# Masked attention with a rational feed-forward on one core: weights decoded without a sign operation, half visits that load their query columns alone, V's padding cleared on GpSimd, and a new order

## The chip, the cores and the metric

The kernel runs on one core of a Trainium2 chip. A core has five engines that run in parallel, each with its own queue of instructions in a fixed order: PE (matrix products; the profile shows its weight loads apart, as PEld), DVE (VectorE), ACT (ScalarE), POOL (GpSimd) and SP (SyncE), which here only issues transfers. The metric is the time of the launch in microseconds of the device, the median of several runs.

## The reference

Attention over 8 batches of 8 heads, 576 positions of 64 values, in which all scores further than tau below their row's maximum are dropped, and a feed-forward layer with a rational function in the middle:

```python
scores = scale * np.matmul(q, k.transpose(0, 1, 3, 2))
thresh = np.max(scores, axis=-1, keepdims=True) - tau
scores = np.where(scores >= thresh, scores, -1000000000.0)
scores = scores - np.max(scores, axis=-1, keepdims=True)
attn = np.exp(scores)
attn = attn / (np.sum(attn, axis=-1, keepdims=True) + 1e-09)
x = np.matmul(attn, v)          # then laid out as 4608 rows of 512
...
h = x @ w_in                    # 512 to 2048
P = a[0] + a[1] * h + a[2] * h2 + a[3] * h3
Q = 1.0 + np.abs(b[0]) * np.abs(h) + np.abs(b[1]) * h2
out = (P / (Q + 1e-06)) @ w_out # 2048 to 512
```

The two weight matrices are handed over as 64-bit floating-point words, which the kernel turns into 32-bit ones itself. Everything else is 32-bit.

## The kernel before

**Attention.** Heads are taken in pairs, 4 pairs to a batch, 32 in all. A pair's 576 rows are four tiles of 128 and a rest of 64; a pair of heads and a tile make a unit. For a unit PE forms the scores (L806, the rest L796), DVE takes the negated maximum (L814), ACT or DVE makes the threshold from it and tau (L821, L823), ACT applies it with a Prelu of a huge slope (L829) and takes the exponential with its sum (L833). The sum is scaled on ACT or DVE (L838, L840) and inverted on DVE (L844). For most units the result is then split into a high and a low half-precision part (high by `times`, L343 on ACT and L345 on DVE; low on DVE, L855), both are transposed by DMA from SP's queue (L865), and PE multiplies them with V (L924). In the first batch many units go another way: DVE scales the identity by the inverted sums (L871), PE transposes by a product with it (L878, L883), `copy` brings the result out (L335 on ACT, L337 on DVE), and PE multiplies in 32 bits (L908). The result is split again into x (L934 or L936, L940).

**Visits.** A pair is not worked through at once. In each batch, three pairs are visited for tiles 0 and 1, the fourth for all five, and then the three again for tiles 2, 3 and the rest: 7 visits a batch, 56 in all, 24 of each half and 8 whole ones. A visit loads its queries (L651, L652, L654 for the rest) and its keys (L659) into one of two buffers each, from SP's queue. Before the change all visits load all query columns.

**V.** V of a pair of heads lies in one of four buffers of 640 columns: four tiles of 128 and 128 more for the rest, of which each head's half is padded by zeros. The buffer is used again for V's half-precision parts, so from the fifth pair on the padding is set to zero anew, on DVE after the load (two memsets, L712). The load is one large DMA (L688) and two small ones (L692), on SP's queue for the first 8 pairs and on GpSimd's afterwards. ACT or DVE takes the largest value (L703, L701), and V is scaled and split (L343 or L345, L741, L744).

**Weights.** 32 pieces of 128 x 512 words are loaded by GpSimd (L549 for w_in, L585 for w_out) and decoded between the units of the first batches. `f1` multiplies the upper half of the word, read as a 32-bit number, by 2^-112 (`times`: ACT L343, DVE L345). `f2` shifts the lower half right on ACT (L507). `f4` shifts the product left by three bits on DVE (L511), which loses its sign. `f5` puts the sign back on DVE (L515). `f6` adds the lower half by an integer addition on DVE (`tensor_tensor`, L350, an ISA row in the order). w_in is then measured (ACT, L557), scaled and split (`times` into `wi`, and L573), w_out split (`copy` into `wp`, and L596).

**Feed-forward.** It goes in steps of 256 rows of x and 512 hidden columns. 48 products L1041 give h (moved by ACT, L1050), ACT and DVE work the rational function (L1055 to L1083), whose result g is split (`copy`, L335 or L337; DVE, L1091), and 24 products L1100 gather the output (L1111, stored by L1120 on GpSimd's queue or, at the end, on SP's). The steps of the last batch's three parts, 12 of them, follow when attention is done.

**The order.** All operations are first entered in a plan: an engine or a choice of engines (`FLEX`, with a duration for each), a key, what must come before, and the buffers it takes and gives back. `Plan.order` then picks the next operation for each engine by a model of times: the smallest key among those that can start first. Where there is a choice, `PRICE` (`EARLY` before `EARLY_END` on the model's clock) weighs the engines. Two tables, `TURN` and `KIND`, shift the keys, by the unit or step and by the kind of operation. In idle gaps of PE up to 400 us on the model's clock, filler products with the identity (L1240) are put in. The engines then run what this gave them, in that order.

Of the kernel before, what the change touches and what calls it, by code (L numbers as in the profile page):

```python
# [8 lines left out]
F32 = mybir.dt.float32  # L9
# [39 lines left out]
NV = 4  # L49
# [24 lines left out]
FLEX = {"f1": {"ACT": 0.567, "DVE": 0.335}, "f6": {"DVE": 0.6}, "s1": {"ACT": 0.648, "DVE": 0.396},  # L74
# [6 lines left out]
EARLY = {"ACT": 1.4369, "DVE": 3.4200}  # L81
EARLY_END = 714.5248
PRICE = {"ACT": 1.0733, "DVE": 2.2524}

TURN = [
# [208 lines left out]
def masked_attention_rational_ffn(  # L294
# [73 lines left out]
    ctx.enter_context(tc.manual_schedule())  # L368
    nc.scalar.preload_act_table_set("natural_log_exp_and_others")
    cf = const.tile([P, 16], F32, name="cf")  # L370
    nc.sync.dma_start(cf[:, 6:7], tau.partition_broadcast(P))
    cv = cf[:, 8:16]
    passes, taue = cv[:, 2:3], cv[:, 3:4]
    ident = const.tile([P, P], F32, name="ident")
# [908 lines left out]
```

## Time and profile before

| | us |
|---|---|
| median of 3 runs (lowest, highest) | 1292.1 (1291.5, 1294.09) |
| the profiled execution | 1291.3 |
| its span, first to last instruction | 1289.5 |
| mean granted TensorE clock | 0.989 |
| DMA queue of SP, share of the 16 DMA engines' time | 44.8% |
| bytes moved | 145.22 MB |

A group of instructions is shown by line, engine, operation, and what it writes and reads, with count, busy time, the mean duration in nanoseconds, and the idle time of its engine just before it, with what ended most of it. Durations of neighbours on one engine overlap a little, so the means times the counts give more than the engine's busy time. A busy PE is not PE at its peak: matmuls are pipelined, and their ends are modelled. An engine's waits are put down to what came last.

### The profile page before, as it was taken

Reading aid. Unit: us, or ns where it says so; the run is one execution under the profiler, and the core shown is the slowest. Engines: PE = TensorE matmul, PEld = TensorE weight load, DVE = VectorE, ACT = ScalarE, POOL = GpSimd, SP = SyncE. Lnnn points to the kernel's source line nnn. Section 1 sums busy time; section 2 is a strip of 40 time slices with the busy share of each in tenths; the row PEclk is TensorE's granted clock in tenths of the full one; section 3 lists DMA queues with packets and bytes.
Section 4 is the critical chain, followed back from the end, with each engine's and each line's share of the span. In section 5 each row is a group of like instructions: output and inputs, shape, how many; then the busy total and the mean of one; then the engine's idle time right before and its main releaser. Section 6 shows DMA issues by size and latency. Waiting matters only on the chain.

```text
span 1289.5 us, 25792 instructions
## 1 busy us (share of the span) xinstructions
PE 1233.6 (96%) x9668; PEld 966.1 (75%) x9668; DVE 1218.6 (95%) x1935; ACT 1110.6 (86%) x2159; POOL 83.8 (6%) x159
## 2 busy tenths in 40 slices
PE   7889899999999999999999989999899999999998
PEld 6667677777777777777777777777677777778886
DVE  5899999999999999899999899999999999999787
ACT  5899999989999989899999799989889899885564
POOL 1111000001001000001000110011001000000000
PEclk8899999999999999999999999999899999999999
DMA  7444374657566565576464465576655665634000
GB/s 207 133 127 130 108 149 92 107 131 155 118 112 143 111 128 111 94 143 145 107 103 101 92 143 113 107 125 123 144 107 121 130 126 108 132 56 72 18 17 16
DMA packets 340779, 145.22 MB, mean 113 GB/s; under 512 B 313136, under 2 KB 318000, under 8 KB 340656
## 3 DMA queue, kind: packets, MB, share of 16 engines
q1 hardware_dynamic: 329840, 111.27, 44.8%
q0 software_dynamic: 10496, 31.73, 8.1%
q8 instruction: 76, 1.25, 0.4%
q10 hardware_dynamic: 320, 0.59, 0.2%
q14 instruction: 47, 0.39, 0.1%
HBM read 58.85 MB, written 9.44 MB: 53 GB/s over the span
## 4 chain that ended last, share of the span: by engine, by line
PE 26%; DVE 22%; issue 5%; ACT 4%; DMA 2%; SPq 0%; DVEq 0%; ACTq 0%
PE banks L1100 11%; PE banks L1041 8%; DVE e L855 4%; PE banks L806 3%; PE banks L924 3%; DVE t L1077 2%; DVE t L1080 2%; DVE st L814 2%; DVE t L1064 2%; DVE g L1091 2%; DVE t L1083 2%; DVE t L1061 2%; DVE t L1074 2%; DMA pT<-hi 1%; PE banks L796 1%
## 5 line engine op out<-in xcount | busy, mean ns | idle before, releaser
L1100 PE MATMUL banks<-wp,g 128*128 128x512 f32 x1728 | 444.3, 405 | 10.7 <-ACT u L1111 7.1
L1100 PEld LDWEIGHTS banks<-wp,g 128*128 128x128 f32 x1728 | 315.0, 189 | 91.7 <-ACT u L1111 7.8
L1041 PEld LDWEIGHTS <-wi 128*128 128x128 f16 x3456 | 328.9, 98 | 72.0 <-issue 30.1
L1041 PE MATMUL banks<-x,wi 128*128 128x256 f16 x3072 | 359.3, 273 | 10.8 <-ACT t L1050 6.8
L833 ACT ACTIVATE e<-e,cf 128x576 f32<-128x576 f32 x288 | 221.1, 774 | 0.2
L829 ACT ACTIVATE e<-banks,st 128x576 f32<-128x576 f32 x288 | 205.8, 735 | 12.4 <-DVE st L823 10.3
L343 ACT ACTIVATE hi<-e,st 128x576 f16<-128x576 f32 x220 | 168.1, 769 | 51.4 <-DVE st L844 45.2
L855 DVE SCALAR_TENSOR_TENSOR e<-e,st,hi 128x576 f16<-128x576 f32 x252 | 204.0, 810 | 4.2 <-ACT hi L343 3.0
L806 PE MATMUL banks<-KK,QQ 64*128 64x64 f32 (+1 forms) x1024 | 175.7, 454 | 10.9 <-ACT e L829 4.4
L814 DVE TENSOR_REDUCE st<-banks 128x2 f32<-128x1152 f32 x128 | 172.1, 1345 | 11.2 <-PE banks L806 9.8
L806 PEld LDWEIGHTS banks<-KK,QQ 64*128 64x128 f32 x1024 | 115.8, 187 | 81.4 <-issue 47.8
L1050 ACT ACTIVATE t<-banks,hsc 128x512 f32<-128x512 f32 (+1 forms) x192 | 106.0, 575 | 25.1 <-PE banks L1041 17.7
L924 PE MATMUL banks<-pT,V 128*64 128x256 f16 (+1 forms) x2520 | 122.3, 250 | 4.4 <-DMA pT<-e 2.1
L924 PEld LDWEIGHTS <-V 128*64 128x64 f16 x2520 | 104.6, 111 | 24.4 <-issue 19.2
L1077 DVE SCALAR_TENSOR_TENSOR t<-t,co,t 128x1024 f32<-128x1024 f32 (+1 forms) x73 | 92.2, 1263 | 16.9 <-ACT t L1071 16.8
L1068 ACT ACTIVATE t<-t,co 128x1024 f32<-128x1024 f32 (+1 forms) x73 | 82.7, 1132 | 28.1 <-DVE t L1074 27.5
L1091 DVE TENSOR_TENSOR g<-t,g 128x512 fp32r<-128x512 f32 x144 | 94.9, 682 | 1.7 <-ACT g L335 1.5
L1061 DVE SCALAR_TENSOR_TENSOR t<-t,co 128x1024 f32<-128x1024 f32 (+1 forms) x73 | 92.1, 1262 | 2.5 <-ACT t L1050 2.5
L1083 DVE SCALAR_TENSOR_TENSOR t<-t,co,t 128x1024 f32<-128x1024 f32 (+1 forms) x73 | 92.3, 1264 | 0.6
L1074 DVE SCALAR_TENSOR_TENSOR t<-t,co,t 128x1024 f32<-128x1024 f32 (+1 forms) x73 | 92.1, 1262 | 0.2
L1064 DVE SCALAR_TENSOR_TENSOR t<-t,co 128x1024 f32<-128x1024 f32 (+1 forms) x73 | 92.1, 1262 | 0.0
L1080 DVE SCALAR_TENSOR_TENSOR t<-t,t 128x1024 f32<-128x1024 f32 (+1 forms) x73 | 87.8, 1203 | 0.6
(118 smaller groups left out, 1202.5 us busy)
## 6 DMA issues: line engine op xcount, KB each, us to landing
KK<-in_kT_dram SPq DMA_DIRECT2D x108, 144.0 KB, 3.0
t<-in_w_in_dram POOLq DMA_DIRECT2D x16, 512.0 KB, 5.7
t<-in_w_out_dram POOLq DMA_DIRECT2D x16, 512.0 KB, 4.8
QQ<-in_qT_dram SPq DMA_DIRECT2D x56, 144.0 KB, 2.8
QQ<-in_qT_dram SPq DMA_DIRECT2D x56, 128.0 KB, 2.8
out_dram<-u POOLq DMA_DIRECT2D x26, 256.0 KB, 3.7
V<-in_v_dram POOLq DMA_DIRECT2D x24, 256.0 KB, 4.7
pT<-hi SPq DMA_TRANSPOSE x140, 3.3
```

Of the source, the lines that this page charges most:

```text
L343: nc.scalar.activation(dst, src, AF.Identity, scale=factor)
L806: mm = nc.tensor.matmul(s[:, d0:d0 + n], QQ[r, t * P:(t + 1) * P], KK[r, k0:k0 + n], **one)
L814: nc.vector.tensor_reduce(box["st"][:, 0:2], box["both"], AX.X, ALU.max, negate=True)
L829: nc.scalar.activation(ev(hh), box["s"][hh], AF.Prelu, scale=SCALE, bias=box["st"][:, 2 + hh:3 + hh], alpha=STEEP)
L833: nc.scalar.activation(e, e, AF.Exp, scale=passes, accum_out=box["st"][:, 4 + hh:5 + hh])
L855: nc.vector.scalar_tensor_tensor(box["lo"][:, c], ev(hh), box["st"][:, 6 + hh:7 + hh], box["hi"][:, c], ALU.mult, ALU.subtract)
L924: nc.tensor.matmul(dst, V[:, c * P + hh * D:c * P + (hh + 1) * D], rhs, start=c == 0 and n == 0, stop=c == NT and n == 2)
L1041: nc.tensor.matmul(d, wi_tile(c, f0 + j, hl), x[:, c, :], start=c == 0 and n == 0, stop=c == NC - 1 and n == 2)
L1077: nc.vector.scalar_tensor_tensor(box["q"], box["q"], qc, box["i"], ALU.add, ALU.mult)
L1083: nc.vector.scalar_tensor_tensor(box["r"], box["r"], a0, box["q"], ALU.add, ALU.mult)
L1091: nc.vector.tensor_tensor(fr(g[:, 1]), box["r"][:, k * GW:(k + 1) * GW], g[:, 0], ALU.subtract)
L1100: nc.tensor.matmul(acc[tt], fr(g[:, x]), fr(wo[f][y]), start=begins and j == n == 0, stop=ends and j == nb - 1 and n == 2)
```

## The change

`f1` is now always on ACT: a Prelu with the scale 2^-112 and, for negative inputs, the slope -2^32. A negative number so becomes positive with an exponent larger by 32, and the shift left by three bits moves that bit of the exponent into the sign. `f5` is gone, and `f1` is no longer in `FLEX`:

```diff
-            times(box["w"], box["rw"][:, :, 1].bitcast(F32), REBIAS)
+            nc.scalar.activation(box["w"], box["rw"][:, :, 1].bitcast(F32), AF.Prelu, scale=REBIAS, alpha=-2.0 ** 32)
...
-        def f5():
-            t = box["w"].bitcast(I32)
-            nc.vector.scalar_tensor_tensor(t, box["rw"][:, :, 1], -0x80000000, t, ALU.bitwise_and, ALU.bitwise_or)
...
-        o1 = op(FLEX["f1"], 0, key, f1, [l], [ht])
+        o1 = op("ACT", 0.567, key, f1, [l], [ht])
         o2 = op("ACT", 0.568, key, f2, [l])
         o4 = op("DVE", 0.335, key, f4, [o1])
-        o5 = op("DVE", 0.602, key, f5, [o4])
-        o6 = op(FLEX["f6"], 0, key, f6, [o5, o2], (), [ht] if dst is None else [ht, hold])
+        o6 = op(FLEX["f6"], 0, key, f6, [o4, o2], (), [ht] if dst is None else [ht, hold])
```

A visit loads the query columns of its own tiles; tau and the four small operations on it (L385 to L388) come behind the first visit's queries:

```diff
         def ldq():
             QQ = QQs[qh.slot]
-            queue.dma_start(QQ[0:D, 0:S], qT[bb, pr, :, 0:S])
-            queue.dma_start(QQ[D:P, 0:NT * P], qT[bb, pr, :, S + REM:])
+            c0, c1 = min(ts) * P, min((max(ts) + 1) * P, NT * P)
+            queue.dma_start(QQ[0:D, c0:S if NT in ts else c1], qT[bb, pr, :, c0:S if NT in ts else c1])
+            queue.dma_start(QQ[D:P, c0:c1], qT[bb, pr, :, S + REM + c0:S + REM + c1])
             if NT in ts:
                 queue.dma_start(QQ[D:P, S:], qT[bb, pr, :, S:S + REM])
+            if first:
+                load_tau()
```

V's padding is cleared by GpSimd for the pairs whose V it loads, ahead of the load:

```diff
+        zero = None if bp < NV else nc.vector if bp < EARLY_BP else nc.gpsimd
+
+        def f_zero():
+            for hh in range(2):
+                zero.memset(Vs[vhold.slot][hh * D:(hh + 1) * D, NT * P + (1 - hh) * D:NT * P + (2 - hh) * D], 0.0)
+
         def ld():
             t = Vs[vhold.slot]
+            if zero is nc.gpsimd:
+                f_zero()
...
-        if bp >= NV:
+        if zero is nc.vector:
             l = v_loaded[bp] = op("DVE", 0.15, max(q, V0 + V1 * pr), f_zero, [l])
```

The tables and prices are others, some 430 numbers:

```diff
-EARLY = {"ACT": 1.4369, "DVE": 3.4200}
+EARLY = {"ACT": 1.2686, "DVE": 3.3582}
-PRICE = {"ACT": 1.0733, "DVE": 2.2524}
+PRICE = {"ACT": 0.8038, "DVE": 2.3173}
...
-    -752, -4167, -3369, 460, -829, -1129, -1318, 524, -372, -1803, -727, -460, -323, 277, -2038, -63, 358, 277, 325,
+    -22753, 3745, 43, -7018, -4551, -3960, -7042, -2152, -4958, -4167, -1023, -845, -1748, -2460, -1722, -1546, 64,
```

So every engine's order is another. Counted over the whole program, DVE has these fewer or more: L515 32 to 0, `times` of the decoding (L345) 16 to 0, memsets 56 to 8, casts of g (L337) 48 to 29, casts of w_out 5 to 13, scalings of w_in (L345) 5 to 13, thresholds (L823) 71 to 61. What has a choice and left DVE is on ACT, and the reverse; the 32 Prelus of `f1` stand there for 16 `times`. GpSimd has 48 memsets more, PE 60 filler products in place of 90.

DVE where the first weights are decoded, before; `u` holds the product of `f1`, `t` the loaded words, and the ISA row is `f6`:

```order
L345 TENSOR_SCALAR u_75<-t_69 128x512
L701 TENSOR_REDUCE vm_272<-V_159 128x1
L511 TENSOR_SCALAR u_75<-u_75 128x512
L871 TENSOR_SCALAR u_74<-ident,st_84 128x128
L515 SCALAR_TENSOR_TENSOR u_75<-t_69,u_75 128x512
L871 TENSOR_SCALAR u_74<-ident,st_84 128x128
L350 ISA t_69<-t_69,u_75 128x512x2
L345 TENSOR_SCALAR u_76<-t_70 128x512
L844 RECIPROCAL st_85<-st_85 128x2
L511 TENSOR_SCALAR u_76<-u_76 128x512
```

The same engine and place now, under the new numbers of the lines (L516 is `f4`, L352 `f6`, L878 the scaled identity):

```order
L516 TENSOR_SCALAR u_74<-u_74 128x512
L516 TENSOR_SCALAR u_76<-u_76 128x512
L352 ISA t_69<-t_69,u_74 128x512x2
L352 ISA t_70<-t_70,u_76 128x512x2
L878 TENSOR_SCALAR u_74<-ident,st_86 128x128
L516 TENSOR_SCALAR u_75<-u_75 128x512
L878 TENSOR_SCALAR u_74<-ident,st_86 128x128
L352 ISA t_71<-t_71,u_75 128x512x2
```

Three rows for a piece (or four, where `f1` was on DVE) have become two, and two pieces are decoded back to back, their `f1` being ACT's.

SP's queue at the start of the program, before:

```order
L371 DMA cf<-in_tau_dram 128x1
L651 DMA QQ_111<-in_qT_dram 64x576
L652 DMA QQ_111<-in_qT_dram 64x512
L688 DMA V_159<-in_v_dram 128x4x128
L692 DMA V_159<-in_v_dram 64x64 x2
L688 DMA V_160<-in_v_dram 128x4x128
L692 DMA V_160<-in_v_dram 64x64 x2
L651 DMA QQ_112<-in_qT_dram 64x576
```

And now (L652 and L653 load queries, L388 tau, L699 and L703 V):

```order
L652 DMA QQ_110<-in_qT_dram 64x256
L653 DMA QQ_110<-in_qT_dram 64x256
L388 DMA cf<-in_tau_dram 128x1
L652 DMA QQ_111<-in_qT_dram 64x256
L653 DMA QQ_111<-in_qT_dram 64x256
L699 DMA V_154<-in_v_dram 128x4x128
L703 DMA V_154<-in_v_dram 64x64 x2
L699 DMA V_155<-in_v_dram 128x4x128
```

Tau went behind the first visit's queries, the second visit's queries went ahead of V's first loads, and each of the first two visits loads 256 columns for each head.

GpSimd's queue where its loads of V begin, behind the last loads of weights, before:

```order
L688 DMA V_162<-in_v_dram 128x4x128
L692 DMA V_162<-in_v_dram 64x64 x2
L1120 DMA out_dram<-u_74 128x512
L1120 DMA out_dram<-u_75 128x512
L1120 DMA out_dram<-t_73 128x512
L688 DMA V_161<-in_v_dram 128x4x128
```

And now (L693 is the memset, L1127 the store of a result):

```order
L1127 DMA out_dram<-u_74 128x512
L1127 DMA out_dram<-u_76 128x512
L693 MEMSET V_155 64x64 x2
L699 DMA V_155<-in_v_dram 128x4x128
L703 DMA V_155<-in_v_dram 64x64 x2
L693 MEMSET V_157 64x64 x2
L699 DMA V_157<-in_v_dram 128x4x128
L703 DMA V_157<-in_v_dram 64x64 x2
```

Two memsets stand ahead of each load of V, and the first stores of results went ahead of the first loads.

More of the change, by code (lines that the diff above doesn't have):

```diff
@@ L72 @@
 RECENT = 9.0
-FLEX = {"f1": {"ACT": 0.567, "DVE": 0.335}, "f6": {"DVE": 0.6}, "s1": {"ACT": 0.648, "DVE": 0.396},
+FLEX = {"f6": {"DVE": 0.6}, "s1": {"ACT": 0.648, "DVE": 0.396},
         "s2": {"DVE": 0.663}, "vmax": {"ACT": 0.697, "DVE": 0.729}, "thr": {"ACT": 0.242, "DVE": 0.122},
@@ L370, in masked_attention_rational_ffn @@
     cf = const.tile([P, 16], F32, name="cf")
-    nc.sync.dma_start(cf[:, 6:7], tau.partition_broadcast(P))
     cv = cf[:, 8:16]
@@ L384, in masked_attention_rational_ffn, with load_tau @@
     KKs = [const.tile([P, S], F32, name=f"KK{i}") for i in range(NQ)]
-    nc.vector.tensor_scalar(passes, cf[:, 6:7], 0.0, None, ALU.is_ge)
-    nc.vector.tensor_scalar(cv[:, 4:5], cf[:, 6:7], 0.0, ALL, ALU.is_lt, ALU.mult)
-    nc.vector.tensor_scalar(taue, cf[:, 6:7], 0.0, 80.0, ALU.max, ALU.min)
-    nc.vector.tensor_tensor(taue, taue, cv[:, 4:5], ALU.add)
+    def load_tau():
+        nc.sync.dma_start(cf[:, 6:7], tau.partition_broadcast(P))
+        nc.vector.tensor_scalar(passes, cf[:, 6:7], 0.0, None, ALU.is_ge)
+        nc.vector.tensor_scalar(cv[:, 4:5], cf[:, 6:7], 0.0, ALL, ALU.is_lt, ALU.mult)
+        nc.vector.tensor_scalar(taue, cf[:, 6:7], 0.0, 80.0, ALU.max, ALU.min)
+        nc.vector.tensor_tensor(taue, taue, cv[:, 4:5], ALU.add)
     b0, b1 = cv[:, 0:1], cv[:, 1:2]
@@ L661, in load_ops @@
         issue = {"DMA": 1.25, "GD": 1.1}[eng]
-        q_done[bp] = [op(eng, 3.1 if first else issue + (0.6 if NT in ts else 0.0), p0, ldq, (), [qh], wire=(0.75, 1.0))]
+        q_done[bp] = [op(eng, 1.8 if first else issue + (0.6 if NT in ts else 0.0), p0, ldq, (), [qh], wire=(0.75 if len(ts) > 3 else 0.4, 1.0))]
         k_done[bp] = [op(eng, 0.1 if act else issue, p0 + 0.1, ldk, (), [kh], wire=(0.75, 1.0))]
@@ L705, in load_v_ops @@
         q = bp * (NT + 0.5) - 17.0
-        l = v_loaded[bp] = op(eng, 1.7, max(q, V0 + V1 * pr), ld, (), [vhold], wire=(0.95, 1.5 if eng == "DMA" else 2.5))
+        l = v_loaded[bp] = op(eng, 1.7 if bp < EARLY_BP else 2.0, max(q, V0 + V1 * pr), ld, (), [vhold], wire=(0.95, 1.5 if eng == "DMA" else 2.5))
         hv = [Hold("u", 1)]
-        def f_zero():
-            for hh in range(2):
-                nc.vector.memset(Vs[vhold.slot][hh * D:(hh + 1) * D, NT * P + (1 - hh) * D:NT * P + (2 - hh) * D], 0.0)
-        if bp >= NV:
+        if zero is nc.vector:
             l = v_loaded[bp] = op("DVE", 0.15, max(q, V0 + V1 * pr), f_zero, [l])
```

48 rows, old and new, of tables (KIND, TURN) are left out of this document.

## The prediction

> **What bounds the kernel now.** I read the page's first lines, then busy time in four stretches, then who waits for whom in the longest of them.
>
> The page's span and busy shares, one entry for each engine:
>
> ```profile
> span 1289.5 us, 25792 instructions
> PE 1233.6 (96%) x9668; PEld 966.1 (75%) x9668; DVE 1218.6 (95%) x1935; ACT 1110.6 (86%) x2159; POOL 83.8 (6%) x159
> ```
>
> Three engines are nearly full, so a share over the span decides nothing. The stretches are those of the work: start-up (0 to 64 us), attention of the first batch beside the decoding of the weights (64 to 200), attention beside the feed-forward (200 to 1180), and the feed-forward alone (from 1180). The columns are busy time and instructions of PE, its weight loads, DVE, ACT and POOL, then granted clock, DMA share and GB/s:
>
> ```profile
> 0.00:64.00 64.00, 52.54 (x325) 43.13 (x326) 46.00 (x121) 46.20 (x104) 11.21 (x33) 0.87 0.59 171
> 64.00:200.00 136.00, 123.44 (x957) 94.90 (x955) 131.75 (x280) 129.50 (x273) 11.01 (x22) 1.00 0.47 126
> 200.00:1180.00 980.00, 953.43 (x7745) 743.06 (x7745) 955.45 (x1447) 879.84 (x1696) 61.54 (x104) 0.99 0.60 118
> 1180.00:1289.50 109.50, 104.19 (x646) 84.98 (x644) 85.44 (x90) 55.04 (x90) 0.00 (x0) 1.00 0.05 15
> ```
>
> From 64 to 200 us DVE idles 4.3 us and ACT 6.5: both are the bound. From 200 to 1180 DVE idles 24.5 us of 980, PE 26.6 by its records, ACT 100. The tail has PE busy for 104 of 109.5 us. Busy rows can't tell DVE from PE in the third stretch; the waits can. Each engine's longest waits there (who waited, for whom, us, times, longest):
>
> ```profile
> DVE t L1077 <- ACT t L1071: 4.5, 5, 2.4
> ...
> ACT hi L343 <- DVE st L844: 45.2, 59, 2.0
> ACT st L821 <- DVE st L814: 13.7, 18, 3.8
> ...
> PE banks L1100 <- ACT u L1111: 7.1, 2, 5.5
> PE banks L1041 <- ACT t L1050: 5.6, 6, 1.4
> ```
>
> ACT waits for DVE in 59 us of its 100 idle; DVE's longest cause is 4.5. So DVE sets the pace for 980 us, with PE close behind, and what leaves DVE there shortens the run nearly one for one until PE's 26.6 us of slack are used.
>
> **The change, part by part.** The prices first: groups of both engines (count, then busy us, mean ns of one, idle before):
>
> ```profile
> L515 DVE SCALAR_TENSOR_TENSOR u<-t,u 128x512 int32<-128x512 int32 x32 | 21.5, 684 | 0.2
> L345 DVE TENSOR_SCALAR u<-t 128x512 f32<-128x512 f32 x16 | 6.5, 417 | 0.9 <-PE banks L883 0.9
> L343 ACT ACTIVATE u<-t 128x512 f32<-128x512 f32 x16 | 10.9, 683 | 0.0
> L337 DVE CAST g<-t 128x512 fp32r<-128x512 f32 x48 | 19.6, 420 | 1.7 <-PE banks L1100 1.2
> L335 ACT CAST g<-t 128x512 fp32r<-128x512 f32 x96 | 56.7, 611 | 11.8 <-DVE t L1083 11.5
> L337 DVE CAST wp<-t 128x512 fp32r<-128x512 f32 x5 | 2.1, 419 | 0.0
> L335 ACT CAST wp<-t 128x512 fp32r<-128x512 f32 x11 | 7.3, 666 | 0.0
> L345 DVE TENSOR_SCALAR wi<-t,sw 128x512 f16<-128x512 f32 x5 | 2.3, 480 | 0.0
> L343 ACT ACTIVATE wi<-t,sw 128x512 f16<-128x512 f32 x11 | 8.4, 776 | 0.0
> ```
>
> A duration overlaps its neighbour's. On DVE's timeline (start, duration) the operation for the sign starts at 46.81 and the next one 0.60 later, though it lasts 0.69; the two memsets of a V tile hold DVE for 0.30:
>
> ```profile
> 46.81 0.69 DVE L515 SCALAR_TENSOR_TENSOR u<-t,u 128x512 int32<-128x512 int32 x1
> 47.41 0.68 DVE L596 TENSOR_TENSOR wp<-t,wp 128x512 fp32r<-128x512 f32 x1
> ...
> 259.45 0.28 DVE L712 MEMSET V<- 64x64 f32 x2
> 259.75 1.28 DVE L1083 SCALAR_TENSOR_TENSOR t<-t,co,t 128x1024 f32<-128x1024 f32 x1
> ```
>
> So I take 0.08 us off every mean when an instruction comes or goes.
>
> *Decoding (up to 200 us).* DVE loses 32 signs at 0.60, 19.2 us, and 16 rescalings at 0.34, 5.4. The new order gives it 8 more casts of w_out at 0.34 (2.7) and 8 more scalings of w_in at 0.40 (3.2), which leave ACT. Net on DVE: 18.7 us less. ACT gains 16 rescalings at 0.60 (9.6) and loses 8 at 0.59 and 8 at 0.70 (10.3): no change within a microsecond. The rescaling is now a Prelu with a slope of -2^32 for negative inputs; no row shows it in this form; the nearest is the Prelu of the scores, with a scale, a bias per row and more elements:
>
> ```profile
> L829 ACT ACTIVATE e<-banks,st 128x576 f32<-128x576 f32 x288 | 205.8, 735 | 12.4 <-DVE st L823 10.3 <-issue 0.9
> ```
>
> It bounds the new one from above, at 52 ns more for each of 32, 1.7 us; I keep 683 ns, since 512 elements are what the old one had. Since DVE and ACT bound this stage together and only DVE is relieved, the stage can shrink by at most what ACT idles there: 6.5 us from 64 on, and some part of 17.8 before. Bounds: 0 and 18.7. I take 8, nearest to ACT's 6.5.
>
> *V's padding.* 48 of 56 memsets leave DVE, 24 pairs at 0.30, all from 200 us on: 7.2 us. GpSimd does them instead, ahead of the three loads of the tile (first row below: the first such load starts at 254 us). It waits there already for the slot (second row), so no new wait arises; behind it are queued those loads and the stores of results. Its own memsets are the price from above, and a tiny operation of GpSimd's shows how long one can be held up (min, median, max ns):
>
> ```profile
> L688 POOL DMA_DIRECT2D V<-in_v_dram x24: 759/788/796, 254.0 to 1038.7; - x24
> ...
> POOL V L688 <- PE banks L924: 337.4, 21, 41.5
> ...
> L632 POOL MEMSET V<- x4: 204/205/205, 1.5 to 2.0; 128x128 f32 x4
> ...
> L496 POOL TENSOR_SCALAR cf<-t x9: 180/180/797, 13.2 to 143.5; 1x1 f32<-1x1 f32 x9
> ```
>
> A V load comes 0.4 us later in a queue that waited 337 us for slots: nothing, unless DVE is disturbed. If each memset stopped a DVE instruction for its own 205 ns, that would be 48 x 0.205 = 9.8 us lost on DVE in place of 7.2 won. The trace can't show it, since GpSimd's memsets of like length have all run by 2.0 us, before DVE has work. The Trainium skill, page "SBUF — State Buffer", section "Who interferes with whom", speaks against the move: GpSimd and some DVE operations (casts and operations with a scalar, between SBUF tiles) share one port pair as an exclusive lock, and whoever comes second is held for the whole instruction. By it, as an estimate, some of the 9.8 would be paid; it is a rival below. I take 0.5 of 9.8 us, since casts and scalings are few among DVE's groups after 200 us.
>
> *The new order after 200 us.* Of 144 casts of g, 19 go from DVE to ACT: 19 x 0.34 = 6.5 us off DVE. Of the thresholds 10 go to ACT,
>
> ```profile
> L821 ACT ACTIVATE st<-st,cf 128x2 f32<-128x2 f32 (+1 forms) x89 | 25.6, 288 | 16.9 <-DVE st L814 16.2 <-DVE st L816 0.3
> L823 DVE TENSOR_SCALAR st<-st,cf 128x2 f32<-128x2 f32 (+1 forms) x71 | 16.0, 225 | 0.3
> ```
>
> which takes 10 x 0.145 = 1.4 off DVE and puts 2.1 on ACT; a handful of others that move both ways come to nothing within a microsecond, on DVE, and to 1 more on ACT. With the padding, DVE has 7.2 + 6.5 + 1.4 = 15 us less, 14.5 after GpSimd's share. ACT gets 19 x 0.53 = 10.1 and those 3, 13 of its 100 idle us. I take 13 of DVE's 14.5 as time, the rest being left to PE's and ACT's narrower slack; bounds 0 (another engine holds the stage) and 15.
>
> *Queries and tau.* SP's first issues, the first wait for queries, and the first scores (start, duration):
>
> ```profile
> 0.74 0.40 SPq L371 DMA_DIRECT2D cf<-in_tau_dram  x1
> 1.49 0.58 SPq L651 DMA_DIRECT2D QQ<-in_qT_dram  x1
> ...
> 8.09 0.60 SPq L651 DMA_DIRECT2D QQ<-in_qT_dram  x1
> ...
> 7.52 0.19 POOL L492 TENSOR_SCALAR cf<-QQ 128x1 f32<-128x1 f32 x1 [2.11 <-DMA QQ<-in_qT_dram]
> ...
> 7.81 1.78 PE L806 MATMUL banks<-KK,QQ 64*128 64x64 f32 x10
> ```
>
> The scores start 0.3 us after the queries land. The queries are now issued 0.75 us earlier and carry half as much, so the start gains 0.75 at least; GpSimd's first weight loads, behind its check of the same queries, gain as much. The second visit's queries, issued at 8.09 behind two tiles of V, move ahead of them. Tau lands later, but its first use follows the first maximum, more than a microsecond after the scores: hidden, and if it weren't, ACT's threshold would wait. The loads (size and us to landing) and PE's wait for them in all:
>
> ```profile
> QQ<-in_qT_dram SPq DMA_DIRECT2D x56, 144.0 KB, 2.8
> QQ<-in_qT_dram SPq DMA_DIRECT2D x56, 128.0 KB, 2.8
> ...
> L806 PE MATMUL banks<-KK,QQ 64*128 64x64 f32 (+1 forms) x1024 | 175.7, 454 | 10.9 <-ACT e L829 4.4 <-DMA KK<-in_kT_dram 3.6 <-DMA QQ<-in_qT_dram 2.9
> ```
>
> In 48 of 56 visits 144 + 128 KB become 64 + 64 or 80 + 64. PE waits 2.9 us for queries and 3.6 for keys that stand behind them; 0.75 to 6 us are the bounds for all of this. I take 2: the 0.75, and under half of the 2.9, since the buffers of the scores may hold PE instead. SP's transposes stand behind shorter transfers, which costs nothing. The filler matmuls fall from 90 to 60; they fill PE's gaps alone, and 0 is their price unless the clock, already 0.87 in the first stretch, falls further.
>
> *The tail.* Same steps, same engines; PE fills 104 of 109.5 us. 0.
>
> Sum: 2 + 8 + 13 = 23 us off the span of 1289.5, so 1266.5. The profiled execution took 1291.3, 1.8 over its span, and the median of the runs is 1292.1, 0.8 over that: 1266.5 + 2.6 = **1269 us**.
>
> **The rivals.**
>
> *A, the forecast: ACT holds the decoding, DVE's relief pays later.* 1262 to 1280. For it: the 6.5 us of ACT from 64 to 200, and the 59 us in which ACT waits for DVE later.
>
> *B, all of DVE's relief is time.* Then 2 + 18.7 + 15 = 36 us: 1256, with a band from 1250 to 1262. It needs ACT to be freed in the decoding by being better fed: both engines' sum there falls by 18.7 us, half for each if the order shares it. Against it: PE's 953 of 980 us. That row is weighed otherwise by the Trainium skill, page "Perfetto Trace Analysis", section "Identifying the Most-Contended Engine": a busy matmul row is a bad measure, one is to go by the time of the weight loads. By the profile's first row of engines that is 75%, and PE would be no bound; the trace agrees in so far as none of the longest waits shown above is for PE.
>
> *C, GpSimd's memsets stop DVE.* The 7.2 become -9.8: 17 us worse than the forecast, 1286. It decides if most memsets meet a cast or scaling on DVE.
>
> *D, PE is the next bound.* If PE can use only 4 of its 26.6 idle us, the decoding gives 2 and the start 1, the gain is 7: 1285.
>
> *E, slower: ACT is the bound.* ACT gets 13 us more after 200 us. If its 100 idle us there are gaps between dependent steps that can't be filled, they stay and the stage grows by 13; with nothing won in the decoding: 1289.5 + 13 - 2 + 2.6 = 1303. It decides once ACT stops waiting for DVE and DVE waits for ACT instead, from 4.5 us to over 20. Against it: 59 of the 100 are waits for the very DVE that is relieved.
>
> **How the numbers follow.** A 0.57, B 0.20, C 0.05, D 0.09, E 0.09. The likeliest is A's 1269. From 1254 to 1287 lie A, two thirds of B, half of C and two thirds of D, about 0.8. What a measurement of this kernel can tell from no change is 0.2%, 2.6 us, so faster means under 1289.5: A, B, C and most of D, 0.87; the same 0.04, from D and E; slower 0.09.
>
> **What would show it.** In the changed profile DVE should be busy some 1185 us (1218.6 - 18.7 - 15), ACT some 1123. The first scores should start near 7.0 us. The last decoding operation on DVE stands so now (count, then first and last start):
>
> ```profile
> L350 DVE CUSTOM_DVE_ANT_0 t<-t,u x32: 666/683/717, 17.8 to 191.1; 128x1024 uint16<-128x1024 uint16 x32
> ```
>
> It should come some 8 us sooner than 191, ACT's idle time up to there nearly gone. Between there and the last attention DVE should idle about 25 us still, ACT wait less than 45 us for the reciprocals, and the tail last 109 us. Right for B: the decoding ends over 15 us sooner. Wrong by C: DVE's casts or scalings with a longer maximum where GpSimd's memsets run. By D: PE over 98% from 200 us on. By E: DVE waiting for ACT by tens of microseconds. If DVE's idle time grows by as much as its work falls, the sum's main step is wrong.

## The result, and the profile after

The changed kernel takes **1275.15 us** (median of 4 runs, 1274.26 to 1278.31) against 1291.8 us for the kernel before beside it (4 runs, 1290.09 to 1294.09): a ratio of 0.9873, with a 95% interval of 0.9851 to 0.9896. That is 16.4 us faster by the ratio (16.7 by the medians) where 23 were forecast (1269, range 1254 to 1287). The profiled execution took 1275.78 us. The page's span and busy shares after:

```profile
span 1273.9 us, 25622 instructions
PE 1226.4 (96%) x9608; PEld 958.5 (75%) x9608; DVE 1188.1 (93%) x1830; ACT 1122.5 (88%) x2184; POOL 91.7 (7%) x206
```

DVE was to be busy some 1185 us and ACT some 1123: 1188.1 and 1122.5. So the work moved as the prediction counted it. DVE lost 30.5 us of work and the span lost 15.6, so DVE's idle time grew by 14.9. Busy time in the same four stretches, in the prediction's columns (the last attention now ends at 1164.4, not 1180):

```profile
0.00:64.00 64.00, 49.94 (x306) 39.62 (x306) 40.91 (x112) 45.84 (x102) 10.38 (x31) 0.87 0.53 154
64.00:200.00 136.00, 128.77 (x1027) 100.96 (x1027) 130.36 (x275) 134.59 (x285) 12.63 (x23) 1.00 0.48 132
200.00:1164.40 964.40, 943.87 (x7608) 732.44 (x7605) 933.64 (x1358) 883.70 (x1705) 68.70 (x152) 0.99 0.57 113
1164.40:1273.90 109.50, 103.78 (x680) 85.52 (x674) 83.22 (x88) 58.39 (x94) 0.00 (x0) 1.00 0.05 15
```

DVE idles 23.1, 5.6, 30.8 and 26.3 us in them; before it was 18.0, 4.3, 24.5 and 24.1. ACT now idles 1.4 us from 64 to 200 (6.5 before). The tail lasts 109.5 us as before.

Cuts at fixed times don't compare equal work, since the order is another. A cut that nearly does is the 25th maximum over a full unit: in both kernels 1632 of the 1728 output products are then still to come, and the 32 pieces are decoded (the changed kernel has done one rest's maximum and 30 products of attention more by then, some 7 us of PE). The row of that maximum on DVE's timeline before (start, duration):

```profile
225.36 1.34 DVE L814 TENSOR_REDUCE st<-banks 128x2 f32<-128x1152 f32 x1
```

Before, the stretches on both sides of it:

```profile
0.00:225.36 225.36, 200.17 (x1479) 156.96 (x1480) 202.90 (x429) 199.07 (x420) 22.21 (x55) 0.96 0.50 135
225.36:1289.50 1064.14, 1033.44 (x8192) 809.10 (x8189) 1015.75 (x1508) 911.52 (x1739) 61.54 (x104) 1.00 0.54 108
```

Before, the output products behind it, as a group:

```profile
L1100 PE MATMUL banks<-wp,g 128*128 128x512 f32 x1632 | 419.3, 405 | 10.1 <-ACT u L1111 7.1 <-DVE g L1091 2.6 <-DVE g L337 0.3
```

The same three of the changed kernel, the maximum first:

```profile
215.49 1.34 DVE L821 TENSOR_REDUCE st<-banks 128x2 f32<-128x1152 f32 x1
```

The stretches on both sides:

```profile
0.00:215.49 215.49, 194.20 (x1454) 152.87 (x1455) 186.72 (x408) 194.19 (x411) 23.01 (x54) 0.96 0.50 135
215.49:1273.90 1058.41, 1032.16 (x8157) 805.67 (x8154) 1001.41 (x1425) 928.34 (x1773) 68.70 (x152) 1.00 0.52 103
```

And the products behind it:

```profile
L1107 PE MATMUL banks<-wp,g 128*128 128x512 f32 x1632 | 421.9, 406 | 7.4 <-ACT u L1118 3.6 <-DVE g L1098 3.1 <-ACT g L337 0.5
```

Up to there 16.2 us of DVE's work left and 9.9 us of time; from there on 14.3 us of work and 5.7 us of time. Behind the cut PE's idle time fell from 30.7 to 26.3 us and ACT's from 152.6 to 130.1, while DVE's grew from 48.4 to 57.0. The forecast of 10 us (2 + 8) for the first part came true, that of 13 for the second did not. This split rests on one execution of each kernel. The granted clock is the same in both on each side (0.96 and 1.00 in the rows). Other profiles of the same program up to there (the experiments with GpSimd's memsets) have the maximum at 221.76 us before and at 212.00 to 213.71 after. So the first part gained 6 to 13 us, and the second 3 to 10 of the 16.4: below 13 in each case.

DVE's waits behind the cut, of before:

```profile
DVE t L1077 <- ACT t L1071: 16.8, 10, 2.8
...
DVE e L855 <- ACT hi L343: 3.0, 4, 1.8
...
DVE st L814 <- PE banks L806: 1.7, 5, 0.6
```

And of after (the first row is mostly the tail's in both):

```profile
DVE t L1084 <- ACT t L1078: 17.8, 10, 2.4
DVE e L862 <- ACT hi L345: 7.4, 10, 1.6
DVE st L821 <- PE banks L813: 4.8, 13, 0.7
DVE st L823 <- PE banks L803: 3.1, 8, 0.5
```

DVE waits 4.4 us more for ACT's high half, 3.1 more for the scores and 3.1 more for the scores of the rests, for which the list of before has no row: together 10.6 us, somewhat more than its idle time grew (8.6).

### The profile page after: what moved, and what is told of

Same layout as the page of the kernel before. It is cut to its first block, busy times and chain, and to the rows that moved or that the text cites. A ratio compares the mean times of both kernels' runs of the same rounds, so it can differ in the third digit from the quotient of the medians.

```text
span 1273.9 us, 25622 instructions
## 1 busy us (share of the span) xinstructions
PE 1226.4 (96%) x9608; PEld 958.5 (75%) x9608; DVE 1188.1 (93%) x1830; ACT 1122.5 (88%) x2184; POOL 91.7 (7%) x206
## 4 chain that ended last, share of the span: by engine, by line
PE 42%; issue 19%; DVE 18%; ACT 5%; DMA 4%; POOL 1%; SPq 0%; DVEq 0%; ACTq 0%; POOLq 0%
PE banks L1107 16%; PE banks L1048 13%; PE banks L813 6%; PE banks L931 6%; DVE e L862 3%; DMA V<-in_v_dram 2%; DVE st L821 2%; DMA pT<-e 2%; DVE t L1071 2%; DVE t L1068 2%; DVE t L1084 2%; DVE g L1098 2%; DVE t L1081 1%; DVE t L1087 1%; PE banks L803 1%
## 5 line engine op out<-in xcount | busy, mean ns | idle before, releaser
L813 PE MATMUL banks<-KK,QQ 64*128 64x512 f32 (+1 forms) x1024 | 178.1, 460 | 14.7 <-ACT e L836 8.4
L345 ACT ACTIVATE hi<-e,st 128x576 f16<-128x576 f32 x222 | 168.9, 768 | 24.5 <-DVE st L851 19.5
```

Of the source, the lines that this page charges most:

```text
L345: nc.scalar.activation(dst, src, AF.Identity, scale=factor)
L813: mm = nc.tensor.matmul(s[:, d0:d0 + n], QQ[r, t * P:(t + 1) * P], KK[r, k0:k0 + n], **one)
```

## The experiments

All were timed beside the kernel before. "Old order" is the kernel before with one edit, "new order" the changed kernel with one edit.

| kernel | median us (lowest, highest) | ratio to before (95%) |
|---|---|---|
| old order, no sign operation | 1289.42 (1287.43, 1294.5) | 0.9993 (0.998, 1.0005) |
| old order, queries and tau as changed | 1287.97 (1286.62, 1292.79) | 0.9978 (0.9966, 0.999) |
| old order, padding on GpSimd | 1288.0 (1286.02, 1293.19) | 0.9974 (0.9962, 0.9987) |
| old order, these three together | 1282.52 (1281.64, 1284.48) | 0.9935 (0.9921, 0.995) |
| new code, old tables and prices | 1344.49 (1342.55, 1354.82) | 1.0431 (1.0401, 1.0461) |
| new order, sign operation back | 1296.51 (1291.91, 1300.91) | 1.0035 (1.002, 1.0051) |
| new order, no lower half on ACT | 1274.77 (1269.82, 1276.23) | 0.986 (0.9838, 0.9882) |
| new order, no shift on DVE | 1274.4 (1270.67, 1281.67) | 0.9864 (0.9836, 0.9892) |
| new order, four times the memsets ahead of the load | 1297.57 (1291.58, 1303.04) | 1.0039 (1.002, 1.0058) |
| new order, memsets behind the load | 1275.68 (1274.19, 1278.08) | 0.988 (0.986, 0.99) |
| new order, four times the memsets behind the load | 1277.87 (1273.56, 1280.87) | 0.9883 (0.9861, 0.9906) |
| new order, a and b loaded early | 1276.49 (1272.17, 1282.64) | 0.9887 (0.9864, 0.991) |

My theory at first was the prediction's: DVE's relief is the gain, and part of it is held back by ACT in the decoding. The rivals were that the gain is the order's alone, that GpSimd's memsets eat a part, and that a stall near 25 us eats a part.

### The sign operation, in the old order

```diff
-            nc.vector.scalar_tensor_tensor(t, box["rw"][:, :, 1], -0x80000000, t, ALU.bitwise_and, ALU.bitwise_or)
```

The weights lose their sign.

> The kernel before, in its own order, with the sign operation left out (the weights lose their sign, nothing else changes): 19.2 us less on VectorE. If VectorE alone is the bound: 19 us less, 1273. If ScalarE shares the bound in the decoding, as the forecast had it: 5 to 9 us less, 1283 to 1287. If the gain of the change came from the new order and not from the work taken away: under 3 us.

The medians differ by 2.6 us, and the interval of the ratio holds no change: "under 3 us", the third case, and not the 5 to 9 of the case that I held. The stretch from 64 to 200 us without the sign:

```profile
64.00:200.00 136.00, 125.27 (x975) 97.02 (x972) 121.88 (x257) 130.27 (x274) 11.24 (x22) 1.00 0.47 126
```

DVE idles 14.1 us there, not 4.3, and ACT is as full as before (130.3 us against 129.5). DVE's longest wait in this stretch is for ACT's lower half, and most of its others there are for ACT too:

```profile
DVE t L350 <- ACT t L507: 2.2, 4, 1.2
```

The 25th maximum on DVE's timeline without the sign:

```profile
221.84 1.34 DVE L814 TENSOR_REDUCE st<-banks 128x2 f32<-128x1152 f32 x1
```

That is 3.5 us sooner than before (225.36), at the same granted clock up to there (0.96 in both), and 0.96 us of it stood already at the first scores (6.85 us against 7.81), ahead of any decoding. So of 19 us less work on DVE at most 2.6 became time, and DVE waits for ACT instead: ACT held the decoding.

The kernel with its padding on GpSimd (below) runs the same program as before up to 250 us, sign operation included, and has this maximum here:

```profile
221.76 1.34 DVE L817 TENSOR_REDUCE st<-banks 128x2 f32<-128x1152 f32 x1
```

So two executions of one program differ by 3.6 us at this point (225.36 against 221.76). Their granted clock in the first 64 us differs too, 0.87 and 0.92. Differences of profiles below that say little unless the clock is the same; the medians do.

### Queries and tau, and the padding, in the old order

```diff
+            c0, c1 = min(ts) * P, min((max(ts) + 1) * P, NT * P)
+            queue.dma_start(QQ[0:D, c0:S if NT in ts else c1], qT[bb, pr, :, c0:S if NT in ts else c1])
...
+            if first:
+                load_tau()
```

> The kernel before, in its own order, with the half loads of queries and tau behind the first of them, and nothing else. The forecast gave 2 us for it, bounds 0.75 and 6. In the old order the second visit's queries still stand behind two tiles of V, so 1 to 2 us less: 1290. If nothing else is late, the first scores start at 7.0 us instead of 7.8.

2.8 us faster by the ratio (0.1 to 0.34%), where the sum had 2.

```diff
+            if bp >= EARLY_BP:
+                for hh in range(2):
+                    nc.gpsimd.memset(t[hh * D:(hh + 1) * D, NT * P + (1 - hh) * D:NT * P + (2 - hh) * D], 0.0)
...
-            for hh in range(2):
+            for hh in range(2 if bp < EARLY_BP else 0):
```

> The kernel before, in its own order, with the 48 memsets of V's padding on GpSimd ahead of the loads instead of on VectorE behind them. 7.2 us less on VectorE: if they count one for one, 1285; with TensorE close behind, 3 to 7 us less. If GpSimd's memsets stop VectorE, or V comes late, no gain or up to 5 us more.

3.4 us faster by the ratio (0.13 to 0.38%), for 5.3 us less of DVE's busy time (1218.6 to 1213.3). Its profile can't show where: it leads by 3.6 us before its first edit acts.

### The three edits together, in the old order

> The kernel before, in its own order, with all three edits (no sign operation, padding on GpSimd, half loads of queries and tau behind them; the weights lose their sign). If the work taken away makes the gain, this has most of the change's 16 us: 12 to 16 us less than before. If the new order makes it, 8 us less or not that. If the new order costs something, more than 16 us less.

8.4 us faster, near the "8 us less" of the case in which the new order makes the gain; the three parts give 0.9 + 2.8 + 3.4 = 7.1, so they add up. Its stretch of the decoding:

```profile
64.00:200.00 136.00, 126.01 (x988) 97.95 (x990) 122.09 (x253) 130.27 (x270) 11.13 (x22) 1.00 0.47 124
```

DVE idles 13.9 us and ACT 5.7. The changed kernel has 5.6 and 1.4 in the same stretch: what was taken away became room, and the new order fills it. The last 7 to 8 us (7.4 by the medians, 1282.52 to 1275.15) are the new order's, with `f1` on ACT for all pieces and its 19 casts of g moved there.

### The new code with the old tables

```diff
-EARLY = {"ACT": 1.2686, "DVE": 3.3582}
+EARLY = {"ACT": 1.4369, "DVE": 3.4200}
-PRICE = {"ACT": 0.8038, "DVE": 2.3173}
+PRICE = {"ACT": 1.0733, "DVE": 2.2524}
...
```

`TURN` and `KIND` are the old ones too, without the number of `f5`.

> The changed code with the old tables and prices, so planned anew by the old shifts. If the order is tuned to the work it holds, this is worse than the changed kernel's 1275 by 5 to 15 us: 1280 to 1290. If the tables hardly matter, 1273 to 1278.

53 us slower than before by the medians (4.0 to 4.6%) and 69 slower than the changed kernel, far more than the 5 to 15 expected. Its stretch of the decoding:

```profile
64.00:200.00 136.00, 121.12 (x972) 95.20 (x972) 113.64 (x244) 130.53 (x275) 12.28 (x23) 1.00 0.42 120
```

DVE idles 22.4 us and PE 14.9 there. Most of the 69 us is lost later: the 25th maximum comes at 226.85 us, 11 late. Its granted clock is lower behind that, 0.97 against 1.00, and what that costs was not separated from the order. The numbers are fitted to one set of operations and prices, and give a bad order for another. So neither half of the change stands alone: the edits in the old order give half of the gain, the old numbers with the new code a loss.

### The sign operation put back, in the new order

```diff
             nc.vector.tensor_single_scalar(t, t, 3, ALU.logical_shift_left)
+            nc.vector.scalar_tensor_tensor(t, box["rw"][:, :, 1], -0x80000000, t, ALU.bitwise_and, ALU.bitwise_or)
```

> The changed kernel with the sign operation put back behind the shift, 32 operations of 0.60 us on VectorE, 19.2 us of work, the order of all else kept. If VectorE alone is the bound, the run grows by 19: 1294. If VectorE and ScalarE share the decoding, VectorE's 5.6 idle us between 64 and 200 us and part of its 23 before take some of it: 8 to 14 us more, 1283 to 1289. If ScalarE holds the decoding, under 5 us.

21 us slower than the changed kernel, for 32 operations that take 19.2 us by the prediction's price: the first case, DVE as the bound. The decoding's stretch:

```profile
64.00:200.00 136.00, 117.69 (x901) 88.77 (x900) 130.88 (x276) 121.63 (x258) 12.44 (x23) 0.99 0.43 121
```

DVE stays full, ACT falls from 134.6 to 121.6 us and PE from 128.8 to 117.7: ACT waits for DVE, and PE for both. The 25th maximum:

```profile
232.32 1.33 DVE L822 TENSOR_REDUCE st<-banks 128x2 f32<-128x1152 f32 x1
```

It is 16.8 us late (232.32 against 215.49). In this order the operation costs about its own time; in the old one 2.6 us at most. Nor does the order alone give the gain, since with the sign in it this kernel is slower than before.

### Less work on ACT, and less on DVE, in the new order

Without the lower half: `f2` goes, 32 operations of ACT, and `f6` takes one operand (the weights lose their lower bits).

```diff
-            nc.scalar.activation(box["rw"][:, :, 0], box["rw"][:, :, 0].bitcast(U32), AF.Copy, scale=2.0 ** -29)
```

> The changed kernel without f2: ScalarE no longer shifts the lower half of the weights' words, and f6 combines the upper half with itself instead of adding the lower one, so the weights are cut to their upper half; 32 operations of 0.6 us leave ScalarE, 19 us, the order of all else kept. If ScalarE alone holds the decoding of the changed kernel (1.4 idle us from 64 to 200): 8 to 14 us less, 1261 to 1267. If VectorE is as tight there as ScalarE (5.6 idle us, and its sign operation cost 21 us when put back): 6 us less at most.

Without the shift: `f4` goes, 32 operations of 0.42 us on DVE.

```diff
-            nc.vector.tensor_single_scalar(t, t, 3, ALU.logical_shift_left)
```

> The changed kernel without the shift (L516) on VectorE: 32 operations of 0.42 us, 13.5 us less of VectorE's work, all between 18 and 167 us; the weights' exponents are then not restored, so part of the decoding is left out; the order is otherwise the changed kernel's. With the sign's operation in this order 19.2 us more of VectorE's work cost 21 us; with the lower half's ScalarE operation out, 19 us less of ScalarE's work gave nothing. If VectorE sets the decoding's pace in this order in both directions, the time falls by 10 to 13 us (about 1264) and VectorE's idle time between 64 and 200 us stays near 6 us. If the order was fitted so that VectorE, ScalarE and TensorE all fill this stage (the theory now), removed work can't be used: at most 3 us are gained (1272 to 1276), VectorE's idle time between 64 and 200 us grows to 12 us or more, and ScalarE stays at 134 of 136 us. In the first case the next wait would be ScalarE's for VectorE; in the second VectorE's for ScalarE or for TensorE's scores.

Both are within their intervals of the changed kernel (0.986 and 0.9864 against 0.9873). The decoding without the lower half:

```profile
64.00:200.00 136.00, 130.60 (x1036) 102.17 (x1032) 131.32 (x276) 126.16 (x263) 13.58 (x23) 1.00 0.49 133
```

ACT idles 9.8 us where it idled 1.4, and DVE is full. Without the shift:

```profile
64.00:200.00 136.00, 130.10 (x1030) 101.59 (x1029) 125.08 (x252) 134.73 (x283) 12.01 (x23) 1.00 0.48 133
```

And DVE's longest wait in that stretch (us, times, longest):

```profile
DVE t L352 <- ACT t L512: 3.4, 6, 1.2
```

Here DVE idles 10.9 us, not quite the 12 expected, and ACT is full. Whichever engine is relieved waits for the other. So "DVE sets the pace", as the run with the sign back suggested by itself, is only half of it: both do, and work added to DVE is paid while work taken from either one is not, the order being kept. A kernel with both relieved at once, which by this account would gain, was not made.

### GpSimd's memsets

```diff
             if zero is nc.gpsimd:
-                f_zero()
+                for _ in range(4):
+                    f_zero()
```

> The changed kernel with each of GpSimd's memsets of the padding done four times: 144 more at 0.145 us, 21 us more of GpSimd. If GpSimd stops VectorE's casts and scalings by a shared port, VectorE's groups get longer maxima and the run grows by 5 us or more. If not, it stays within 2 us of 1275, since GpSimd waits hundreds of microseconds for free buffers.

22 us slower than the changed kernel, where "within 2 us" or a disturbed DVE had been expected. This looked like rival C. But DVE's casts had a median of 420 ns as before, and ACT waited for V. So the memsets were moved behind the three loads of a tile, once as they are and once fourfold:

```diff
-            if zero is nc.gpsimd:
-                f_zero()
...
+            if zero is nc.gpsimd:
+                for _ in range(4):
+                    f_zero()
```

> The changed kernel with GpSimd's two memsets of the padding behind the three loads of a V tile instead of ahead of them, all else in order. In the changed kernel's trace a load is issued 0.58 us after its memsets begin, 24 times, and ScalarE waits 7.6 us for V. If V's loads are on the path, as the fourfold memsets suggest (22 us for 24 delays of 1.2 us), the run gets 3 to 8 us shorter: 1267 to 1272, a version faster than both. If the memsets cost by keeping GpSimd or a port busy, nothing changes: 1274 to 1277.

> The fourfold memsets again, behind the three loads. If only the loads' delay costs, this is within 3 us of the single memsets behind the loads. If GpSimd's work as such costs (a port shared with VectorE, stores that come late), it is as slow as the fourfold memsets ahead of the loads: 1290 or more.

Neither differs from the changed kernel (0.988 and 0.9883 against 0.9873), so the 3 to 8 us expected of the single ones did not come. The fourfold memsets ahead of the load (count, shortest, median and longest in ns, first and last start):

```profile
L693 POOL MEMSET V<- x192: 145/147/436, 265.1 to 1042.7; 64x64 f32 x192
```

DVE's casts of g in that kernel, in the same columns:

```profile
L339 DVE CAST g<-t x29: 403/420/662, 133.3 to 1216.4; 128x512 fp32r<-128x512 f32 x29
```

ACT's wait for V from 200 us on:

```profile
ACT u L715 <- DMA V<-in_v_dram: 35.5, 15, 6.4
```

And GpSimd's timeline at the first of these tiles:

```profile
265.05 1.55 POOL L693 MEMSET V<- 64x64 f32 x8 [25.16 <-PE banks L932]
266.83 0.76 POOL L700 DMA_DIRECT2D V<-in_v_dram  x1 [0.23 <-issue]
```

Fourfold behind the load, the groups of memsets and casts:

```profile
L693 POOL MEMSET V<- 64x64 f32 x192 | 29.0, 151 | 10.0
L339 DVE CAST g<-t 128x512 fp32r<-128x512 f32 x29 | 11.7, 423 | 0.2
```

And ACT's wait for V there:

```profile
ACT u L715 <- DMA V<-in_v_dram: 11.0, 7, 3.5
```

As the change has them, the casts:

```profile
L339 DVE CAST g<-t 128x512 fp32r<-128x512 f32 x29 | 11.7, 421 | 0.2
```

ACT's wait for V:

```profile
ACT u L714 <- DMA V<-in_v_dram: 7.6, 8, 2.1
```

And GpSimd's timeline at its first tile:

```profile
268.91 0.33 POOL L693 MEMSET V<- 64x64 f32 x2 [25.50 <-PE banks L931]
269.49 0.76 POOL L699 DMA_DIRECT2D V<-in_v_dram  x1 [0.24 <-issue]
```

Behind the load, 29 us of memsets cost nothing that the runs can tell (0.9883, 0.9861 to 0.9906, against 0.9873). Ahead of the load they put it off: by 0.58 us as changed, by 1.78 fourfold, and then ACT waits 35.5 us for V in place of 7.6. The price of the memsets is the load's delay: nothing measurable at 0.58 us, 22 us for 24 tiles at 1.78. The granted clock is lower too with the fourfold memsets ahead of the load (0.982 to 0.988 in its runs, 0.988 to 0.991 in the changed kernel's); whether a part of the 22 us is the clock's was not tried.

The two engines do meet at times. One of the fourfold memsets ahead of the load began while DVE scaled a high half (first DVE's timeline, then GpSimd's):

```profile
445.03 0.51 DVE L347 TENSOR_SCALAR hi<-e,st 128x576 f16<-128x576 f32 x1
445.19 0.44 POOL L693 MEMSET V<- 64x64 f32 x1
```

That memset took 436 ns in place of 147. In the two fourfold kernels 8 of the 384 memsets took 314 to 535 ns, and each of the 8 began during such a scaling or a cast of g on DVE. The scalings and casts themselves were not stopped: no DVE instruction beside a memset lasted over 0.08 us longer than the median of its kind. The cast of 662 ns stands beside GpSimd's issue of a load (0.80 us from 308.13), not beside a memset.

### The stall near 25 us

The changed kernel's longest waits in the first 64 us include this one, at about 27 us:

```profile
ACT cf L405 <- DMA cf<-in_b_dram: 6.1, 1, 6.1
```

ACT waits for the load of b, and DVE 6.0 us for ACT. The loads of a and b went to ACT's queue, behind the first keys:

```diff
+                nc.scalar.dma_start(cf[:, 0:4], a.partition_broadcast(P))
+                nc.scalar.dma_start(cf[:, 4:6], b.partition_broadcast(P))
```

> The changed kernel, with one thing moved: the two loads of the coefficients a and b go out on ScalarE's queue behind the first keys instead of on SyncE's at 19.5 us. In the changed kernel's trace ScalarE waits 6.1 us for b at 26.9 us and VectorE 6.0 us behind it. If that wait is what the start-up lost, the run gets 3 to 6 us shorter than the changed kernel (1275 us): 1269 to 1272. If the start-up is held by the third visit's keys and queries (TensorE waits 4.0 and 1.5 us for them at 23.3 and 25.5 us), the run gains 1 us at most.

No gain (0.9887 against 0.9873). The wait for b is gone, and among the longest of the first 64 us are now these:

```profile
DVE st L853 <- ACT st L847: 6.6, 1, 6.6
...
PE banks L815 <- DMA KK<-in_kT_dram: 4.9, 2, 4.4
```

DVE now waits as long for a sum of ACT's, and PE for keys: b had been late beside other things that were late.

## Why the prediction was right and where it was wrong

**The likeliest case came out in its number**: 1275 lies in A's band (1262 to 1280). Its mechanism came out by half. That ACT held the decoding is shown by the old order without the sign, and ACT's wait for the reciprocals fell from 45.2 to 19.5 us (forecast: under 45). But "DVE's relief pays later" did not hold: 5.7 us came later, and 9.9, the greater part, in the start and the decoding, where it took the new order. In the changed kernel ACT no longer holds the decoding alone.

**The step that failed** is the one on which the term of 13 rests: "what leaves DVE there shortens the run nearly one for one until PE's 26.6 us of slack are used". The work was counted rightly (14.3 us left DVE behind the cut, 14.5 forecast), but only 5.7 became time, with 26.3 of PE's 30.7 us still idle. I took idle time as slack that can be used up. Instead DVE's own idle time grew by 8.6 us, over half of the work that left it, which comes near the prediction's sign for a wrong main step. DVE's waits for ACT's high half went from 4 to 10, of 1.6 us at most, and those for PE's scores from 5 to 21, of 0.7 us at most. Nor does PE's idle time lie free: a wait for ACT's exponentials is its longest behind the cut, and it grew. Before:

```profile
PE banks L806 <- ACT e L829: 3.5, 4, 2.5
```

And after:

```profile
PE banks L813 <- ACT e L836: 6.5, 8, 2.9
```

By its size this is what D described (PE uses only 4 of its idle time: 4.4 measured), in this part of the program alone; but PE stayed just under D's sign of 98% (943.87 of 964.40 us, 97.9%). Whether PE, or ACT with its 16.8 us more of work there (911.5 to 928.3), holds DVE behind the cut was not tried; it would take a kernel with less work on one of them after 215 us. This stays open. One part of the term paid better: in the old order the padding gave 3.4 us for 5.3 of DVE's time.

**Decoding, 8 with bounds 0 and 18.7: right in size.** Start and decoding together gave 9.9 us. The reason held in the old order: DVE's relief alone could not be used while ACT was full. What I had not seen is that both halves are needed: the removal of the sign in the old order gives 2.6 us at most, the new order with the sign in it is slower than before. So the right size of 8 was in part luck: ACT's 6.5 idle us, from which I took it, were the old order's. The sign that I gave for this step was wrong. The last decoding operation (count, first and last start):

```profile
L352 DVE CUSTOM_DVE_ANT_0 t<-t,u x32: 680/693/706, 18.9 to 166.8; 128x1024 uint16<-128x1024 uint16 x32
```

came 24 us sooner, not 8, and so beyond the 15 that were to speak for B, because the new order puts decoding ahead of units. The end of one kind of work is no clock when the order changes.

**The Prelu of f1**: 0.683 us kept, and its row has 22 ns more, 0.7 us over 32. Of the 22 ns, 15 were added to the unchanged shift of the lower half as well (689 to 704), so only a part can be the Prelu's:

```profile
L509 ACT ACTIVATE u<-t 128x512 f32<-128x512 f32 x32 | 22.5, 705 | 0.0
```

**Padding**: the 0.5 us for a disturbed DVE should have been about 0, and rival C is refuted as priced: beside memsets DVE lost under 0.08 us at a time. Its sign, a longer maximum of the casts (662 ns), did appear, but beside the issue of a load. "A V load comes 0.4 us later in a queue that waited 337 us for slots: nothing" was right by luck. The queue's wait is for the slot; once the slot is free the load is on the path, with between 0.6 and 1.8 us to spare. The page "SBUF — State Buffer" of the Trainium skill, section "Who interferes with whom", has GpSimd and some of DVE's casts and scalings hold each other up by a shared port, whoever comes second. The traces agree with it in the 8 memsets of 314 to 535 ns that began beside such an operation; it was GpSimd that waited, and too seldom to cost time.

**Queries and tau**: 2 forecast, 2.8 measured in the old order. The first scores came at 7.22 us (7.0 forecast), but not for the reason given. "The filler matmuls ... 0 is their price" was wrong for the first ones, and "the scores start 0.3 us after the queries land" was a coincidence. The old order without the sign loads its queries as before, and its scores start at 6.85 us, half a microsecond ahead of the same check of the queries on GpSimd (7.35). Before, the first fillers end at 7.88 us, as the scores start (7.81):

```profile
1.37 6.51 PE L1240 MATMUL banks<-ident 128*128 128x128 f32 x34 [1.37 <-POOL ident masks.py:199]
```

The start of the changed kernel:

```profile
1.38 5.91 PE L1247 MATMUL banks<-ident 128*128 128x128 f32 x26 [1.38 <-POOL ident masks.py:199]
7.22 2.49 PE L813 MATMUL banks<-KK,QQ 64*128 64x64 f32 x16
...
5.01 0.18 POOL L497 TENSOR_SCALAR cf<-KK 128x1 f32<-128x1 f32 x1 [2.81 <-DMA KK<-in_kT_dram]
5.28 0.19 POOL L497 TENSOR_SCALAR cf<-QQ 128x1 f32<-128x1 f32 x1
```

Keys and queries have landed by 5.0 and 5.3 us, and tau by 5.25, well ahead of its use. The fillers end at 7.29, so they hold the first scores by about 2 us. A shorter first filling was not tried. In the old order the first scores came at 6.85 to 7.81 us in three profiles without the edit of the queries, and at 6.87 and 7.52 in two with it. So where the 2.8 us come from is not shown; the first scores do not show it.

**E** is refuted by its time (1303) and its own sign: DVE's waits for ACT did not go to over 20 us in one place, the longest outside the tail being 7.4. **B** too: 36 us were not there. **The tail**: 0 forecast and 109.5 us in both.

## What to carry to other kernels

In a program whose engines run fixed orders and are all over 85% busy, count work removed from one engine as time only where the order can be fitted anew, and not one for one (here 16.4 us for 30.5); test it from both sides, by adding work and by removing it, since here, in the new order, adding to DVE cost its full time and removing from DVE or ACT gave nothing. An engine's idle time is not slack as long as it is waits for the other engines: ask for whom it waits first. When an operation moves to another queue, price what it puts off there (a load behind a freed slot) before what it might disturb.

## What the runs showed of the hardware

- A memset of 64x64 takes 146 ns on GpSimd; one that begins beside a scaling or a cast on VectorE took 314 to 535 ns (8 of 384).
- The start differs between executions of one program, by 3.6 us at the 25th maximum. A likely source is the granted clock: it falls to half for spells of 3.4 us or a multiple of it, and their number differs. One of 6.8 us, in the profile of before:

```profile
27.00:33.80 6.80, 6.55 (x26) 5.40 (x27) 4.59 (x13) 3.33 (x8) 0.00 (x0) 0.50 0.07 22
```

That profile has 17.0 us at half clock in the first 64 us, and the old order with the padding on GpSimd 10.2; the difference is worth 3.4 us of a full PE, as an estimate.
- The first fillers are another source, and the granted clock does not show why. The same 26 records take 5.91 us in the changed kernel and 4.96 in the one with the memsets behind the load, 0.23 and 0.19 us a record; the first scores come 1 us sooner there, and the granted clock of the first 7 us is 1.00 in both.
